# A second queue for the first weights: tile 1 of x sent behind tile 0, k's weights over two DMA queues, b1 and b2 sent after pair 10

## The chip, the cores and the metric

The kernel runs on one core of one Trainium2 chip. The metric is device time in microseconds, lower is better. The kernel before takes 485.36 us (median of three runs, 485.15 to 486.0). In the profile the engines are named PE (TensorE; PEld is its weight load), DVE (VectorE), ACT (ScalarE), POOL (GpSimd) and SP (SyncE). DMA transfers are issued by SP and by ACT, each with a queue of its own: q1 is SP's and q10 ACT's. Both run on the core's 16 DMA engines.

## The reference

One layer over 2048 positions of width 512, all in fp32:

```python
xn = layernorm(x)                                   # over the last axis, no gain
q, k, v = split(xn @ wqkv)                          # 32 heads of 16
logits = einsum(q, k at pos - 2*w, w = 0..7) / 4    # 8 keys, every second position back
attn = softmax(where(pos - 2*w >= 0, logits, -1e9))
s = einsum(attn, v at the same positions) @ wo
h = relu(xn @ w1 + b1) ** 2                         # 1792 hidden
g = silu(h @ w2 + b2)
out = x + s * g
```

x is (1, 2048, 512), wqkv (512, 1536), wo (512, 512), w1 (512, 1792), w2 (1792, 512), b1 (1792), b2 (512).

## The kernel before

**Precision.** Each large product is made of fast matmuls on a high part and a low part: every operand is split in two (`high` is a copy by ACT that rounds, `low` a subtraction), and three products (high by high, high by low, low by high) stand for one fp32 product. Only the very first product, k of tile 0, takes the fp32 operands as they are, so that it need not wait for splits.

**Phase 1, tiles of x.** x is cut into 16 tiles of 128 rows. A tile is loaded, normalized (statistics by `stats`: DVE, and rs by POOL; then `norm`), transposed, split, and multiplied by the weights of q, k and v. Tiles 0 and 1 are handled by code written out line by line; then come pairs of tiles, a = 2, 4, ... 14. Pairs 4 to 14 use sums of quarters of the tile and of the weights (`pair_of_seven`) to save a product. The q, k, v of a pair are stored to a scratch in DRAM (`store_qkv`: sq, sk, sv), from which attention loads units of 256 positions. Tiles from 4 on also store their transposed, split x to a scratch (sx), for phase 2.

**Attention** runs on DVE beside the products, as a stream of small steps which a planner lets in by estimated clocks of PE and DVE.

**Phase 2, the hidden layer.** For four chunks of 512 positions, blocks f = 0 to 13 of 128 hidden units: `up` makes h (ACT: relu with b1, then squares), `down` adds the product with w2 to four accumulators, which ACT filled with b2 before (`begin`). The first two blocks of chunk 0 lie already in pair 14. The weights of a block are loaded by `load_w` and split by `next_w`, two blocks ahead.

**The head.** The program starts with loads in this order: tile 0 of x, piece 0 of k's weights (rows 0 to 127 of the 512), tile 1, pieces 1 to 3 of k's weights, then q's weights in two halves, tiles 2 and 3, v's weights in two halves. Every one is issued by SP. PE meanwhile runs 18 transposes of the identity (tile `warm`). The chain to the first product is: tile 0 lands, bn_stats and bn_aggr on DVE, rs on POOL, xn in two halves on DVE, four transposes on PE (pxT), two copies on ACT (xT0f), and then k of tile 0 from xT0f and the raw pieces of the weights (pq from wqraw), the transposes of tile 1 between the third and the fourth piece.

**What sets the order.** Work on PE, DVE, ACT and POOL is written in the order in which each engine is to do it (`Ordered` keeps it). A transfer sent with `queue` or `A.dma_start` keeps its place too, on SP's and on ACT's queue. One sent with `dma` is placed by the scheduler: b1 and b2 stand in the code after pair 12 (line 885), but the scheduler issues them behind the first loads, since they wait for nothing. Each DMA issue also takes one of eight semaphores in turn, and waits until the transfer that had it eight issues earlier has landed.

Of the kernel before, what the change touches and what calls it, by code (L numbers as in the profile page):

```python
# [15 lines left out]
P = 128  # L16
S = 2048
D = 512
F = 1792
KT = D // P  # L20
# [39 lines left out]
def body(ctx: ExitStack, tc: tile.TileContext, x, wqkv, wo, w1, b1, w2, b2, out):  # L60
# [34 lines left out]
    PE, V, A, G = Ordered(nc.tensor, "PE"), Ordered(nc.vector, "V"), Ordered(nc.scalar), Ordered(nc.gpsimd)  # L95
# [4 lines left out]
    dma = nc.sync.dma_start  # L100

    def queue(out, in_):

        tc.keep_in_program_order(dma(out, in_))
# [19 lines left out]
    def piece(name):  # L124
        return keep.tile([P, 512], F32, name=name, tag="z", bufs=4)
# [26 lines left out]
    def load_x(t):  # L152
        xins[t] = px.tile([P, D], F32, name=f"x{t}", tag="x", bufs=4)
        queue(xins[t], tile_rows(x, t))
# [6 lines left out]

    raws = {}

    def load_wq(s, kt, tag=None):
        rows = wqkv[kt * P:(kt + (2 if tag else 1)) * P, s * 512:(s + 1) * 512]
        if tag is None:
            raws[s, kt] = piece(f"wqraw{s}_{kt}")
            dma(raws[s, kt], rows)
            return
        if kt == 0:  # L170
            raws[s] = att.tile([P, KT, 512], F32, name=f"wqraw{s}", tag=tag)
        dma(raws[s][:, kt:kt + 2], rows.rearrange("(k p) n -> p k n", p=P))
        for i in (kt, kt + 1):
            raws[s, i] = raws[s][:, i]
# [4 lines left out]


    load_x(0)
    load_wq(1, 0)
    load_x(1)
    for kt in range(1, KT):
        load_wq(1, kt)
    for kt in (0, 2):
        load_wq(0, kt, "pr")
    load_x(2)
# [17 lines left out]
    b1t = const.tile([P, NF], F32, name="b1t")  # L206
    b2t = const.tile([P, D], F32, name="b2t")
# [177 lines left out]
    def pump(margin=-SLACK):  # L385

        limit = clock["PE"] + margin
        flush(clock["PE"])
        while True:
            if coming[0] is None:  # L390
                coming[0] = next(stream, None)
            if coming[0] is None or clock["V"] + coming[0] > limit:
                break
            coming[0] = next(stream, None)
        if coming[0] is None:
            not_before(limit)
# [22 lines left out]
    NT = S // P  # L419
# [460 lines left out]
    for a in range(2, NT, 2):  # L880
        if a >= TPC:
            for t in (a, a + 1):
                queue(sx[t // TPC][:, :, t % TPC], xts[t].bitcast(F32))
        (pair_of_seven if a in SEVEN else pair)(a)
        if a == NT - 4:
            dma(b1t, b1.rearrange("(f p) -> p f", p=P))
            dma(b2t, b2[None, :].to_broadcast([P, D]))
    pump()
    lowh(1)
    p1ctx.close()  # L890
# [76 lines left out]
    for c in range(NCH):  # L967
# [7 lines left out]
        for f in range(2, NF):  # L975
# [4 lines left out]
            if c == 0 and f in (3, 6):  # L980
# [3 lines left out]
                for q in range(4):  # L984
                    rows = wo[q * P + 64 * i:q * P + 64 * i + 64, :].rearrange("(g p) n -> p g n", g=2)
# [105 lines left out]
```

## Time and profile before

| | before |
|---|---|
| median of 3 runs | 485.36 us (485.15 to 486.0) |
| profiled execution, its own time | 485.13 us |
| its span, first to last instruction | 483.1 us |
| granted TensorE clock | 1.00 |
| PE busy | 477.4 us (99%) |
| DVE busy | 423.0 us (88%) |
| first product of the kernel starts at | 6.70 us |
| DMA moved | 81.47 MB, mean 169 GB/s |

Times in the rows are microseconds from the span's start. A row of the timeline gives start, duration, engine, line, operation, the tile written, the tiles read, shapes, and the count where equal neighbours are merged; in brackets the idle time of that engine just before, and what ended it. L91 is the line of a helper through which nearly all instructions are issued, so rows are told apart by their tiles: `x` a tile of x, `wqraw` raw weights of q, k or v, `wq` their split, `st`, `mv`, `rs`, `xn` the steps of the normalization, `pxT` its transpose in PSUM, `xT0f` tile 0's transpose in fp32, `pq` and `pm` accumulators of q, k, v, `ph` and `pb` those of `up` and `down`, `stg` the stage of a store, `sx` the scratch of transposed x, `w1r` and `w2r` raw weights of phase 2. SPq and ACTq are DMA issues. The rows on which the argument rests stand in the prediction.

### The profile page before, as it was taken

What the parts mean: (1) busy time and instruction counts of PE and PEld (TensorE: products, weight loads), DVE (VectorE), ACT (ScalarE), POOL (GpSimd) and SP (SyncE); (2) the same over time, 40 slices, a digit from 0 to 9 for tenths busy, and PEclk for the clock granted to TensorE, in tenths of its full rate; (3) what the DMA queues carried; (4) which work ended last, traced back from release to release, by engine and by line L of the source; (5) the groups of instructions that cost most, each with busy time, mean ns of one, the idle gap of its engine ahead of it and who ended that gap; (6) DMA issues with size and microseconds to landing.
All of it is one profiled execution on the core that took longest, in us unless ns stands there. A gap on an engine that the chain in (4) does not pass through costs nothing.

```text
span 483.1 us, 6128 instructions
## 1 busy us (share of the span) xinstructions
PE 477.4 (99%) x2190; PEld 396.6 (82%) x2190; DVE 423.0 (88%) x352; ACT 240.0 (50%) x441; POOL 225.3 (47%) x178
## 2 busy tenths in 40 slices
PE   8999999999999999999999999999999999999996
PEld 5888888888888888888888888888888888888885
DVE  5978999899499899999999999999999999889133
ACT  5548798856566565273513345342234543423240
POOL 1459853116986699436543322434433345253210
PEclk9999999999999999999999999999999999999999
DMA  7899999998779996571627548071707725220321
GB/s 283 243 251 258 277 243 302 263 306 269 209 198 228 255 224 151 178 166 43 170 72 185 115 164 190 26 189 43 197 16 196 224 48 145 43 86 27 87 105 71
DMA packets 71002, 81.47 MB, mean 169 GB/s; under 512 B 6204, under 2 KB 55612, under 8 KB 70972
## 3 DMA queue, kind: packets, MB, share of 16 engines
q1 hardware_dynamic: 65788, 54.87, 41.3%
q10 hardware_dynamic: 5184, 26.22, 21.8%
q8 instruction: 17, 0.28, 0.2%
q14 instruction: 13, 0.11, 0.1%
HBM read 50.60 MB, written 27.32 MB: 161 GB/s over the span
## 4 chain that ended last, share of the span: by engine, by line
PE 98%; DMA 1%; DVE 0%; POOL 0%; issue 0%; ACT 0%; POOLq 0%
PE ph L91 32%; PE pb L91 32%; PE pm L91 12%; PE pq L91 9%; PE pw L91 9%; PE pv L91 4%; DMA x<-in_A_x 1%; PE pxT L91 0%; DVE z L91 0%; DVE st L91 0%; POOL rs L91 0%; DVE xn L91 0%; ACT xT0f L91 0%; DVE mv L91 0%; DVE rs L91 0%
## 5 line engine op out<-in xcount | busy, mean ns | idle before, releaser
L91 PE MATMUL pb<-w,h 128*128 128x512 f32 x672 | 160.1, 389 | 0.0
L91 PEld LDWEIGHTS pb<-w,h 128*128 128x128 f32 x672 | 126.1, 188 | 26.2
L91 POOL TENSOR_TENSOR h<-hf,h 128x512 fp32r<-128x512 f32 x46 | 67.7, 1473 | 157.5 <-ACT hf L91 157.5
L91 PE MATMUL ph<-xU,w 128*128 128x512 f32 x504 | 120.2, 389 | 0.0
L91 ACT ACTIVATE ph<-ph,b1t 128x512 f32<-128x512 f32 x56 | 37.0, 661 | 153.9 <-PE ph L91 144.0
L91 PEld LDWEIGHTS ph<-xU,w 128*128 128x128 f32 x504 | 94.6, 188 | 19.6
L91 DVE TENSOR_TENSOR pr<-k,q 128x2048 f32<-128x2048 f32 x32 | 78.7, 2460 | 3.2 <-DMA q<-sq 2.5
L91 DVE TENSOR_TENSOR pv<-v,L 128x2048 f32<-128x2048 f32 x32 | 77.3, 2417 | 3.8 <-POOL L L91 3.1
L91 DVE TENSOR_REDUCE L<-pr 128x128 f32<-128x2048 f32 x32 | 73.0, 2281 | 0.7
L91 DVE TENSOR_REDUCE v<-pv 128x256 f32<-128x2048 f32 x32 | 72.9, 2279 | 0.7
L91 PE MATMUL pw<-wot,oT 128*128 128x512 f32 (+1 forms) x204 | 45.9, 376 | 0.0
L91 PEld LDWEIGHTS pw<-wot,oT 128*128 128x128 f32 x204 | 36.8, 188 | 7.1
L91 POOL TENSOR_TENSOR w<-w1r,w 128x512 fp32r<-128x512 f32 x14 | 31.6, 2259 | 23.4 <-ACT w L91 23.2
L91 PE MATMUL ph<-xT,w 128*128 128x512 f32 x168 | 40.0, 389 | 0.0
L91 PEld LDWEIGHTS ph<-xT,w 128*128 128x128 f32 x168 | 31.5, 188 | 6.6
L91 PE MATMUL pm<-wq,S 128*128 128x512 f32 x144 | 36.8, 392 | 0.0
L91 ACT ACTIVATE h<-ph 128x512 fp32r<-128x512 f32 x56 | 33.5, 599 | 1.8
L91 PE MATMUL pq<-wq,xT 128*128 128x512 f32 x132 | 30.9, 393 | 0.0
L91 PEld LDWEIGHTS pm<-wq,S 128*128 128x128 f32 x144 | 26.2, 188 | 5.3 <-DVE S L91 0.4
L91 PEld LDWEIGHTS pq<-wq,xT 128*128 128x128 f32 x132 | 24.5, 188 | 5.9 <-ACT xT L91 0.7
L91 ACT ACTIVATE hf<-ph 128x512 f32<-128x512 f32 x46 | 27.4, 595 | 1.9 <-POOL h L91 1.9
L91 PE MATMUL pm<-wq,xt 128*128 128x512 f32 x108 | 27.6, 392 | 0.0
(96 smaller groups left out, 531.0 us busy)
## 6 DMA issues: line engine op xcount, KB each, us to landing
k<-sk ACTq DMA_DIRECT2D x8, 960.0 KB, 7.1
v<-sv ACTq DMA_DIRECT2D x8, 960.0 KB, 7.4
sx<-xt SPq DMA_DIRECT2D x12, 512.0 KB, 5.8
xU<-sx ACTq DMA_DIRECT2D x12, 512.0 KB, 5.9
x<-in_A_x SPq DMA_DIRECT2D x16, 256.0 KB, 6.4
sk<-stg SPq DMA_DIRECT2D x8, 512.0 KB, 4.3
sq<-stg SPq DMA_DIRECT2D x8, 512.0 KB, 7.5
sv<-stg SPq DMA_DIRECT2D x8, 512.0 KB, 5.0
```

Of the source, the lines that this page charges most:

```text
L91: return tc.keep_in_program_order(f(*a, **k))
```

## The change

Three things are altered:

1. Tile 1 of x is issued directly behind tile 0.
2. The four pieces of k's weights go out on two queues: pieces 0 and 2 are issued by ACT, pieces 1 and 3 by SP, each in a fixed place.
3. b1 and b2 are sent in a fixed place on SP's queue, after pair 10 (NT - 6), instead of by the scheduler from a place after pair 12.

```diff
-    def load_wq(s, kt, tag=None):
+    def load_wq(s, kt, tag=None, send=dma):
         rows = wqkv[kt * P:(kt + (2 if tag else 1)) * P, s * 512:(s + 1) * 512]
         if tag is None:
             raws[s, kt] = piece(f"wqraw{s}_{kt}")
-            dma(raws[s, kt], rows)
+            send(raws[s, kt], rows)
             return
...
     load_x(0)
-    load_wq(1, 0)
     load_x(1)
-    for kt in range(1, KT):
-        load_wq(1, kt)
+    for kt in range(KT):
+        load_wq(1, kt, send=queue if kt % 2 else A.dma_start)
...
         (pair_of_seven if a in SEVEN else pair)(a)
-        if a == NT - 4:
-            dma(b1t, b1.rearrange("(f p) -> p f", p=P))
-            dma(b2t, b2[None, :].to_broadcast([P, D]))
+        if a == NT - 6:
+            queue(b1t, b1.rearrange("(f p) -> p f", p=P))
+            queue(b2t, b2[None, :].to_broadcast([P, D]))
```

SP's first issues before. x_121 is tile 0 of x and x_125 tile 1, wqraw_0 to wqraw_3 are the four pieces of k's weights, wqraw_133 those of q:

```order
L104 DMA x_121<-in_A_x 128x512
L168 DMA wqraw_0_123<-in_A_wqkv 128x512
L104 DMA x_125<-in_A_x 128x512
L168 DMA wqraw_1_127<-in_A_wqkv 128x512
L168 DMA wqraw_2_129<-in_A_wqkv 128x512
L168 DMA wqraw_3_131<-in_A_wqkv 128x512
L172 DMA wqraw_133<-in_A_wqkv 128x2x512 x2
```

SP's first issues of the change (x_123 is now tile 1):

```order
L104 DMA x_121<-in_A_x 128x512
L104 DMA x_123<-in_A_x 128x512
L104 DMA wqraw_1_127<-in_A_wqkv 128x512
L104 DMA wqraw_3_131<-in_A_wqkv 128x512
L172 DMA wqraw_133<-in_A_wqkv 128x2x512 x2
```

Tile 1 moved up behind tile 0, and pieces 0 and 2 left SP's queue. They stand now at the start of ACT's instructions, where before the table load was first:

```order
L91 DMA wqraw_0_125<-in_A_wqkv 128x512
L91 DMA wqraw_2_129<-in_A_wqkv 128x512
L91 ACT_TABLE_LOAD
L91 ACTIVATE wq_113<-wqraw_0_125 128x512
L91 ACTIVATE xT0f<-pxT_0_169 128x256
```

ACT issues both pieces ahead of its table load, and its first work (the split of piece 0) stands behind it as before.

SP's queue before, from pair 10's store of q on. sx_154 is the scratch of transposed x of tiles 12 to 15 (four stores, of xt_1122, xt_1125, xt_1270 and xt_1273), w1r_1325 and w2r_1326 the weights of block 2, w1r_1416 and w2r_1417 those of block 3, and stg_1, stg_2, stg_0 pair 12's stages of k, v and q:

```order
L104 DMA sq<-stg_0_1088 128x8x128
L104 DMA sx_154<-xt_1122 512x1x256
L104 DMA sx_154<-xt_1125 512x1x256
L104 DMA sx_154<-xt_1270 512x1x256
L404 DMA w1r_1325<-in_B_w 128x4x128
L405 DMA w2r_1326<-in_B_w 128x512
L104 DMA sk<-stg_1_1234 128x8x128
L104 DMA sx_154<-xt_1273 512x1x256
L104 DMA sv<-stg_2_1235 128x8x128
L104 DMA sq<-stg_0_1236 128x8x128
L404 DMA w1r_1416<-in_B_w 128x4x128
L405 DMA w2r_1417<-in_B_w 128x512
```

The same place of the change, where the names of these tiles have other numbers (xt_1272 and xt_1275 are tiles 14 and 15, w1r_1327 and w2r_1328 block 2):

```order
L104 DMA b1t<-in_B_b 128x14x1
L104 DMA b2t<-in_B_b 128x512
L104 DMA sx_154<-xt_1122 512x1x256
L104 DMA sx_154<-xt_1125 512x1x256
L403 DMA w1r_1327<-in_B_w 128x4x128
L404 DMA w2r_1328<-in_B_w 128x512
L104 DMA sk<-stg_1_1236 128x8x128
L104 DMA sv<-stg_2_1237 128x8x128
L104 DMA sq<-stg_0_1238 128x8x128
L104 DMA sx_154<-xt_1272 512x1x256
L104 DMA sx_154<-xt_1275 512x1x256
L403 DMA w1r_1416<-in_B_w 128x4x128
```

b1 and b2 stand directly behind pair 10's store of q, and the stores of tiles 14 and 15 have gone behind all three stores of pair 12, directly ahead of the weights of block 3. On PE, DVE and POOL the order of the work is the same in both kernels.

## The prediction

> **What bounds the kernel now.** I read the page first: the busy shares, then the chain that ended last.
>
> ```profile
> span 483.1 us, 6128 instructions
> PE 477.4 (99%) x2190; PEld 396.6 (82%) x2190; DVE 423.0 (88%) x352; ACT 240.0 (50%) x441; POOL 225.3 (47%) x178
> PE 98%; DMA 1%; DVE 0%; POOL 0%; issue 0%; ACT 0%; POOLq 0%
> ```
>
> TensorE is the bound, and nearly alone. So the next question is where it is not working, which the waits of PE answer:
>
> ```profile
> PE warm L91 <- POOL mhalf L91: 1.4, 1, 1.4
> PE pxT L91 <- DVE xn L91: 0.3, 1, 0.3
> PE pq L91 <- ACT xT0f L91: 0.2, 1, 0.2
> ```
>
> These are all its waits in 483 us, and all lie at the start. A few microseconds before the first real product and after the last make the rest. So the change can act in two ways only: it moves the moment at which PE starts on real work, after which the dense stream shifts as a whole, or it makes PE wait somewhere for the first time. The chain in order of time, start us and duration, shows what sets that moment:
>
> ```profile
> 0.73 2.71 DMA x<-in_A_x
> ...
> 3.47 0.70 DVE st L91
> ...
> 5.31 0.42 DVE xn L91
> ...
> 5.78 0.46 PE pxT L91 x2
> ...
> 6.26 0.39 ACT xT0f L91
> ...
> 6.70 2.84 PE pq L91 x6
> ```
>
> From x's tile 0 landing to the first product there is no slack: statistics, rs, xn, four transposes, a copy. Whatever delays tile 0's landing delays everything; whatever lands later than tile 0 matters only if it becomes later than this chain.
>
> **Part 1, the head: tile 1 ahead, k's weights on two queues.** Today one queue carries tile 0, piece 0 of k's weights, tile 1, pieces 1 to 3, in that order. Issues and the waits that end on their landings:
>
> ```profile
> 0.73 0.39 SPq L104 DMA_DIRECT2D x<-in_A_x  x1
> 1.18 0.42 SPq L168 DMA_DIRECT2D wqraw<-in_A_wqkv  x1
> 1.65 0.42 SPq L104 DMA_DIRECT2D x<-in_A_x  x1
> 2.12 1.38 SPq L168 DMA_DIRECT2D wqraw<-in_A_wqkv  x3
> 0.73 1.28 ACT L91 ACT_TABLE_LOAD   x1 [0.73 <-PEq L1080]
> 3.47 0.69 DVE L91 BATCH_NORM_STATS2 st<-x 128x6 f32<-128x512 f32 x1 [3.47 <-DMA x<-in_A_x]
> 4.29 0.63 ACT L91 ACTIVATE wq<-wqraw 128x512 fp32r<-128x512 f32 x1 [2.28 <-DMA wqraw<-in_A_wqkv]
> 6.53 0.69 DVE L91 BATCH_NORM_STATS2 st<-x 128x6 f32<-128x512 f32 x1 [0.48 <-DMA x<-in_A_x]
> 7.23 0.19 PEld L91 LDWEIGHTS pq<-wqraw,xT0f 128*128 128x128 f32 x1 [0.24 <-DMA wqraw<-in_A_wqkv]
> 7.66 0.19 PEld L91 LDWEIGHTS pq<-wqraw,xT0f 128*128 128x128 f32 x1 [0.24 <-issue]
> 9.39 0.63 PE L91 MATMUL pxT<-ident,xn 128*128 128x128 f32 x4
> ```
>
> *What it gains.* Tile 1 lands at 6.5 and ends in its xn, which the transposes at 9.39 need. Ahead of them stand six half products in steps of 0.43 (7.66 - 7.23): the sixth's weights are loaded at 7.23 + 3 x 0.43 = 8.52, it starts a step later and gives way at 9.38. The transposes start at 9.39, and their row has no idle time. So tile 1 costs PE 0.01 or 0.02 us today, and an earlier tile 1 is worth no more: DVE is on xn of tile 0 until shortly before 6.5 in any case. SP also has two issues fewer ahead of its later ones (0.84 us); those bring the weights of q and tiles 2 and 3, for which PE waits in no row.
>
> *What it costs.* Piece 0 no longer stands behind tile 0 in one queue. It goes out on ACT's queue, and in the new order both of ACT's issues stand ahead of its table load, so the first can start at the 0.73 at which the table load starts now: the moment of tile 0's own issue. Two transfers of 256 KB then run side by side on the same 16 engines. Two bounds for what tile 0 loses:
> - Below, 0: tile 0 is served first and piece 0 gets the rest.
> - Above within fair sharing, 0.82: both are in by 4.29 today (4.29 - 3.47 = 0.82 after tile 0), and the last of the pair cannot land later if the same bytes move at the same rate.
>
> A tile of 128 rows of 2 KB is 8 pieces for each of 16 engines. If an engine takes pieces from the two queues in turn, tile 0's last is the 15th of 16 instead of the 8th: 7 of the 8 additional pieces stand ahead of it: 7/8 x 0.82 = 0.72. Is it in turn? The trace has one stretch where tiles of x on SP's queue and the load of q on ACT's share the engines, and one where SP's queue runs alone:
>
> ```profile
> DMA packets 163, 0.46 MB, mean 231 GB/s; under 512 B 7, under 2 KB 7, under 8 KB 163
> q10 hardware_dynamic: 76, 0.29, 59.9%
> q1 hardware_dynamic: 87, 0.18, 38.3%
> DMA packets 412, 0.78 MB, mean 389 GB/s; under 512 B 32, under 2 KB 32, under 8 KB 412
> DMA packets 325, 0.60 MB, mean 300 GB/s; under 512 B 32, under 2 KB 32, under 8 KB 325
> ```
>
> The first three rows are 33 to 35 us (q10 is ACT's queue, q1 SP's), the fourth 7 to 9 us, the last 2 to 4 us. With both queues loaded, 76 and 87 packets went through: about one for one. That is nearest to the fair share, so I take 0.72.
>
> [...]
>
> *What else moves.* ACT's table load starts 2 x 0.42 later and ends near 2.9; ACT's first work is at 4.29, so it is covered, and would cost only if the issues took 1.4 us longer than SP's. With the chain 0.72 later, DVE comes to tile 1's statistics at 6.77 instead of 6.53, so tile 1 may land 0.24 later than now without a wait. Piece 1 is now the third on SP, and the fifth transfer in the engines' common order instead of the fourth; it lands at 7.2 today, and one transfer more is up to 0.82, so at 8.0 or a little before, against a weight load that moves to 7.23 + 0.72 = 7.95. It fits without reserve; I put its price at 0, at most 0.2.
>
> **Part 2, b1 and b2 out of the head.** Both stand in SP's queue behind the first loads:
>
> ```profile
> 9.91 0.38 SPq L886 DMA_DIRECT2D b1t<-in_B_b  x1
> 11.27 4.25 SPq L887 DMA_DIRECT2D b2t<-in_B_b  x1
> 15.62 0.38 SPq L104 DMA_DIRECT2D sk<-stg  x1
> DMA packets 1978, 0.32 MB, mean 159 GB/s; under 512 B 1826, under 2 KB 1826, under 8 KB 1978
> ```
>
> b1 is 1,792 packets of 4 bytes (the last row, 15 to 17 us, shows them), b2 256 KB. Taking them away frees SP for about 4.6 us and the engines for some 2 us (I estimate 1.4 for b1, from the fall to 159 GB/s, and 0.65 for 256 KB at 389). Behind them stands the first store of k (15.62), which can leave earlier. Nothing of it reaches PE, which has no wait behind 6.7 us: gain 0.
>
> **Part 3, b1 and b2 after pair 10.** They now stand behind pair 10's store of q, and past them are queued the four stores of x^T, the weights w1 and w2 of block 2, and pair 12's stores:
>
> ```profile
> 102.21 4.05 SPq L104 DMA_DIRECT2D sq<-stg  x1
> 106.31 3.49 SPq L104 DMA_DIRECT2D sx<-xt  x3
> 114.08 0.38 SPq L404 DMA_DIRECT2D w1r<-in_B_w  x1
> 114.00:116.50 2.50, 2.50 (x15) 2.16 (x14) 2.43 (x4) 0.00 (x0) 2.50 (x3) 1.00 0.39 111
> 128.44 0.64 ACT L91 ACTIVATE ph<-ph,b1t 128x512 f32<-128x512 f32 x1
> 137.08 2.16 ACT L91 ACTIVATE pb<-b2t 128x512 f32<-128x512 f32 x4
> 127.12 0.63 ACT L91 ACTIVATE w<-w1r 128x512 fp32r<-128x512 f32 x1 [1.69 <-DMA w1r<-in_B_w]
> 132.93 0.60 ACT L91 ACTIVATE hf<-ph 128x512 f32<-128x512 f32 x1 [1.54 <-POOL h L91]
> ```
>
> SP has 4.3 us free between 109.8 and 114.08, and the fifth row (a window; its last columns are the DMA share 0.39 and 111 GB/s) shows the engines more than half idle at 114 to 116.5. b1 and b2 put 4.6 us into the first, less one store of x^T of 3.49 / 3 = 1.16 that goes behind pair 12's q now: net 3.5. They fit, 0.8 to spare. First uses are at 128.4 and 137.1, some 10 us after any plausible landing. The place to watch is 127.12: ACT waits there for w1 of block 3, and one store of x^T more (512 KB, 1.35 us at 389 GB/s) now stands between pair 12's stores and it, so it may come 1.3 to 1.5 us later. Behind it ACT stands idle 1.54 us at 132.93, so the delay is used up before it meets PE. Price 0; if that cover were gone, up to 1.5.
>
> **The sum.** +0.72 - 0.02 + 0 + 0 = +0.70. The profiled execution took 485.13 us (span 483.1); +0.70 is 485.83. The median of the runs is 485.36, 0.23 above that execution, so the forecast for the median is 486.06, rounded 486.1. Anything within 0.2% (0.97 us, about what a measurement of this kernel can tell from no change) counts as the same.
>
> **The rivals.**
> - *Shared queues are slower in sum.* At 33 to 35 us both queues together moved 231 GB/s, against 300 at 2 to 4 us and 389 at 7 to 9 us for SP's alone. If sharing itself costs that, 524 KB take 2.27 us instead of 1.75, and tile 0 lands 0.52 later still: +1.24 - 0.02, 486.6. It decides from a shared rate below about 262 GB/s (524 KB in 2.0 us, +0.97). Against it: the load of q in that stretch reads another memory layout than these loads do, and may be slow by itself.
> - *Tile 0 stays whole.* SP's pieces are in the engines first, and piece 0 takes only what they leave. Then the head is as before but for the 0.02: 485.36 - 0.02, 485.3. It needs ACT's first issue to start later than SP's by as much as tile 0 takes, or an engine that does not change queues within 8 pieces. The one-for-one count speaks against the second, but over 2 us it cannot show turns of 8.
>   [...]
> - *b1 and b2 find no room* (+0.5 to +1.5 at 128 to 139 us; 486.4): the spare above is 0.8 us on SP.
> - *Faster.* Two queues keep the engines busier at 2 to 4 us (300 GB/s, where 389 is possible): 524 KB would take 1.35 instead of 1.75, and tile 0 would lose 0.3 instead of 0.72, 485.7. For a real gain tile 0 would have to land before its 3.47, and nothing in the change sends it earlier; the most to win is PE's two waits, 0.5 us: 484.9.
>
> **How the numbers follow.** Forecast (tile 0 loses 0.3 to 0.97): 0.48. Slow sharing: 0.27. Tile 0 whole: 0.14. b1 and b2 in the way: 0.06. Faster: 0.05. Slower by over 0.2% takes slow sharing, half of the b1 case, and the upper edge of the forecast (0.08): 0.38. The last case, as far as it can be worked out, stays within 0.2%; beyond it lies only what this profile does not show, and I leave faster by over 0.2% those 0.05. Same is the rest, 0.57. The range goes from 485.2 (tile 0 whole, with runs that spread by some tenths) to 487.1 (slow sharing, with piece 1 or b1 on top).
>
> **What would show it.** The first statistics of DVE at 4.1 to 4.2 instead of 3.47 with PE's first product at 7.4; packets of q10 among those of the first 2 us; tile 1's statistics without a wait; ACT's table load behind two issues; PE without a wait from 7.4 to the end, at 114 to 139 us above all. The forecast is wrong if the first statistics stay at 3.5 (tile 0 whole), come after 4.5 (slow sharing), or if PE shows a wait that this profile does not have.

## The result

The changed kernel takes 489.06 us (median of six runs, 487.47 to 490.18) against 485.72 (485.15 to 486.01) for the kernel before beside it: a ratio of 1.0069, 95% interval 1.0048 to 1.009. It is 3.3 us slower; the forecast was +0.7, with 487.1 as the upper end. The profiled execution took 489.67 us, 4.54 more than the profiled one of before.

The page of the changed kernel, its span, busy time and chain by engine:

```profile
span 487.9 us, 6126 instructions
PE 480.5 (98%) x2190; PEld 397.1 (81%) x2190; DVE 421.5 (86%) x352; ACT 239.9 (49%) x441; POOL 238.5 (49%) x178
...
PE 85%; POOL 4%; DMA 4%; DVE 3%; issue 3%; ACT 1%; ACTq 0%; SPq 0%; DVEq 0%; POOLq 0%
```

PE was 98% of the chain that ended last and is 85%: POOL, DMA and DVE now stand on it. The waits of PE, and of its weight loads, name two places:

```profile
PE warm L91 <- POOL mhalf L91: 1.4, 1, 1.4
PE pxT L91 <- DVE xn L91: 1.2, 1, 1.2
PE ph L91 <- DVE h L91: 0.7, 1, 0.7
PEld ph L91 <- DVE h L91: 3.1, 6, 1.1
```

The wait ahead of the first transposes (pxT) has grown from 0.33 to 1.21 us, and there are six waits of the hidden layer's weight loads for DVE's h, one of which PE's own row shows too; the profile of before has none of them.

Where the 4.54 us lie can be cut at two instructions that both programs have: the first split product (pq from wq and xT) and the first hidden product (ph from xT). The timeline of PE gives their starts, here of before and then of the changed kernel:

```profile
10.71 3.04 PE L91 MATMUL pq<-wq,xT 128*128 128x512 f32 x12
...
123.99 4.24 PE L91 MATMUL ph<-xT,w 128*128 128x512 f32 x18
```

```profile
13.04 1.20 PE L91 MATMUL pq<-wq,xT 128*128 128x512 f32 x4
...
126.22 1.98 PE L91 MATMUL ph<-xT,w 128*128 128x512 f32 x8
```

The head costs 13.04 - 10.71 = 2.33 us. From there to the first hidden product it is 113.18 against 113.28. From the first hidden product to the start of the last product of the program the traces have 357.50 against 354.99: 2.51 us more. The start of the last product to the end of the span differs by 0.03, and the rest (-0.2) lies outside the span of the profile. So two losses, each of over 2 us in this execution, where one of 0.7 was forecast.

**The head.** The timeline of the changed kernel:

```profile
0.73 0.87 SPq L104 DMA_DIRECT2D x<-in_A_x  x2
0.73 0.89 ACTq L91 DMA_DIRECT2D wqraw<-in_A_wqkv  x2
1.66 1.28 ACT L91 ACT_TABLE_LOAD   x1 [1.66 <-PEq L1079]
4.35 0.69 DVE L91 BATCH_NORM_STATS2 st<-x 128x6 f32<-128x512 f32 x1 [4.35 <-DMA x<-in_A_x]
6.67 1.11 PE L91 MATMUL pxT<-ident,xn 128*128 128x128 f32 x4 [1.21 <-DVE xn L91]
6.85 0.69 DVE L91 BATCH_NORM_STATS2 st<-x 128x6 f32<-128x512 f32 x1
7.83 4.09 PE L91 MATMUL pq<-wqraw,xT0f 128*128 128x512 f32 x6
```

and the DMA view of 0.7 to 4.3 us, packets, MB and share by queue (q1 is SP's, q10 ACT's):

```profile
q1 hardware_dynamic: 234, 0.45, 39.6%
q10 hardware_dynamic: 160, 0.29, 23.3%
```

ACT's first issue does go out at 0.73, together with tile 0's. By the time tile 0 is in, the other queue has moved 160 packets beside SP's 234, where before SP's queue was alone. Tile 0's statistics begin at 4.35 instead of 3.47: 0.88 later, the step that the prediction put at 0.72. The view reaches a little past tile 0; from 0.7 to 3.7 us it has 137 packets of q1 and 116 of q10. The two queues together were also slower than the one queue of before, 234 against 284 GB/s at 1.7 to 3.5 us. But the products then lose more: the first six, 2.84 us before, take 4.09, and the four transposes 1.11 instead of the 0.76 that they took in the kernel before:

```profile
5.78 0.76 PE L91 MATMUL pxT<-ident,xn 128*128 128x128 f32 x4 [0.33 <-DVE xn L91]
```

The view of these products gives the shortest, median and longest of the eight in ns, of before and then of the changed kernel:

```profile
L91 PE MATMUL pq<-wqraw,xT0f x8: 592/592/697, 6.7 to 10.3; 128*128 128x512 f32 x8
```

```profile
L91 PE MATMUL pq<-wqraw,xT0f x8: 592/594/1220, 7.8 to 12.6; 128*128 128x512 f32 x8
```

The same product at up to twice the time, with no row of a wait ahead of it: the clock is the suspect.

**The middle.** In the rows below, of the changed kernel, first ACT, then SP, POOL, DVE and PE, SP sends two stores of x^T (sx) at 122.04, directly ahead of block 3's weights:

```profile
131.31 0.63 ACT L91 ACTIVATE w<-w1r 128x512 fp32r<-128x512 f32 x1 [4.24 <-DMA w1r<-in_B_w]
...
147.56 0.52 ACTq L91 DMA_DIRECT2D k<-sk  x1
...
157.87 0.52 ACTq L91 DMA_DIRECT2D q<-sq  x1
158.50 0.66 ACT L91 ACTIVATE ph<-ph,b1t 128x512 f32<-128x512 f32 x1 [8.80 <-DMA w2r<-in_B_w]
```

```profile
122.04 3.72 SPq L104 DMA_DIRECT2D sx<-xt  x2
...
148.70 0.34 SPq L404 DMA_DIRECT2D w2r<-in_B_w  x1
```

```profile
145.32 3.35 POOL L91 TENSOR_TENSOR w<-w2r,w 128x512 fp32r<-128x512 f32 x1
```

```profile
160.37 0.69 DVE L91 TENSOR_TENSOR h<-ph,h 128x512 fp32r<-128x512 f32 x1 [4.92 <-ACT ph L91]
...
161.12 3.03 PE L91 MATMUL ph<-xT,w 128*128 128x512 f32 x12 [0.70 <-DVE h L91]
```

And in the kernel before, the same two loads of ACT and the load of w2 of SP:

```profile
145.35 0.52 ACTq L91 DMA_DIRECT2D k<-sk  x1
...
147.77 0.52 ACTq L91 DMA_DIRECT2D q<-sq  x1
```

```profile
144.13 0.34 SPq L405 DMA_DIRECT2D w2r<-in_B_w  x1
```

```profile
142.81 1.29 POOL L91 TENSOR_TENSOR w<-w2r,w 128x512 fp32r<-128x512 f32 x1
```

The last row is POOL's split just ahead of that load. Read as a chain, with times counted from the first hidden product (123.99 before, 126.22 now): ACT gets w1 of block 3 at 5.1 instead of 3.1. POOL's splits of the following blocks slip, and the one at 145.32 takes 3.35 us where its counterpart of before took 1.29. That split frees the buffer for the load of w2 of block 7, which SP so issues at 22.5 instead of 20.1 (148.70, 0.03 us after the split's end at 148.67; before 144.13, after 144.10). At 21.3, in both kernels, ACT issues attention's load of k, 960 KB. Before, w2 went ahead of it; now it goes behind, and the DMA view of 150 to 152 us shows ACT's queue alone:

```profile
q10 hardware_dynamic: 60, 0.46, 100.0%
```

In the kernel before the same two microseconds have 52 packets of q10 and 51 of q1, so a load of k does not always keep SP's queue out; what decides is open.

ACT's next load, of q, takes one of the eight semaphores in turn, the one that this w2 still holds. So it is issued at 31.7 instead of 23.8, when w2 has landed (9.2 us after its issue at 148.70); ACT works in order and stands 8.80 us, DVE gets ph late (4.92), and PE waits for h (at 161.12, and five times more until 190). This is the reading of one execution; how far it holds is shown by the experiments.

### The profile page after: what moved, and what is told of

The parts are those of the page before. It is cut to its first block, busy times and chain, and to the rows that moved or that the text cites. A ratio compares the mean times of both kernels' runs of the same rounds, so it can differ in the third digit from the quotient of the medians.

```text
span 487.9 us, 6126 instructions
## 1 busy us (share of the span) xinstructions
PE 480.5 (98%) x2190; PEld 397.1 (81%) x2190; DVE 421.5 (86%) x352; ACT 239.9 (49%) x441; POOL 238.5 (49%) x178
## 4 chain that ended last, share of the span: by engine, by line
PE 85%; POOL 4%; DMA 4%; DVE 3%; issue 3%; ACT 1%; ACTq 0%; SPq 0%; DVEq 0%; POOLq 0%
PE pb L91 27%; PE ph L91 26%; PE pm L91 10%; PE pw L91 9%; PE pq L91 8%; PE pv L91 4%; DMA w2r<-in_B_w 3%; POOL w L91 3%; DVE L L91 1%; DMA x<-in_A_x 1%; POOL stg L91 1%; DVE h L91 1%; ACT ph L91 1%; DVE pv L91 0%; PE pxT L91 0%
## 5 line engine op out<-in xcount | busy, mean ns | idle before, releaser
L91 POOL TENSOR_TENSOR h<-hf,h 128x512 fp32r<-128x512 f32 x46 | 76.6, 1666 | 145.5 <-ACT hf L91 143.0
L91 DVE TENSOR_TENSOR pr<-k,q 128x2048 f32<-128x2048 f32 x32 | 77.7, 2429 | 1.3 <-DMA q<-sq 0.6
L91 POOL TENSOR_TENSOR w<-w1r,w 128x512 fp32r<-128x512 f32 x14 | 36.0, 2572 | 22.1 <-ACT w L91 22.1
```

The source lines that it names most:

```text
L91: return tc.keep_in_program_order(f(*a, **k))
```

## The experiments

Each is told against the kernel before in runs on the same chip. In the profiles three numbers were compared: the start of the first split product (10.71 before), the moment of ACT's copy of block 3's w1 behind the first hidden product (3.1 before), and the time from the first hidden product to the last product (354.99 before).

**The two halves alone.** The head's two edits with b1 and b2 as before, and the move of b1 and b2 with the head as before. The diff of the second:

```diff
-        if a == NT - 4:
-            dma(b1t, b1.rearrange("(f p) -> p f", p=P))
-            dma(b2t, b2[None, :].to_broadcast([P, D]))
+        if a == NT - 6:
+            queue(b1t, b1.rearrange("(f p) -> p f", p=P))
+            queue(b2t, b2[None, :].to_broadcast([P, D]))
```

> Only the head of the change (tile 1 behind tile 0, k's pieces on two queues); b1 and b2 stay where the kernel before has them. Theory A (the loss is two: tile 0 lands 0.9 us late and the wider gap ahead of PE's transposes keeps TensorE's clock low, 2.3 us together at the head; and a separate stall at 160 to 190 us that comes from b1 and b2 standing among pair 10's and 12's stores): the first product of the k accumulator on split weights starts at about 13.0 instead of 10.7, no wait of PE behind 20 us, median about 487.7 (+2.0 to +2.4). Rival B (the stall at 160 us comes from the head's shift alone): the stall shows here too, about 489.5. Rival C (b1 and b2 make the head late): head as before, about 485.6.

> Only b1 and b2 are sent after pair 10; the head is as before. Theory A: first work on split weights at 10.7 as before; ACT waits for w1 of block 3 about 4 us instead of 1.7, the load of q behind 145 us is issued some 8 to 10 us later than before, and PE waits for DVE's low part of h between 155 and 190 us, in sum 2 to 2.4 us: 487.5 to 488. Rival B: no wait of PE at all, 485.4 to 486.

Head alone: 487.26 us against 486.55 (ratio 1.0014, 0.9991 to 1.0037). b1 and b2 alone: 487.66 (1.0018, 0.9997 to 1.0039). Neither is told from no change, and their sum, 0.32%, is not the 0.69% of the whole; in these runs the kernel before stood 0.8 to 1.2 us higher than in the others. The profiles say more. b1 and b2 alone: 10.71 as before, but the copy of w1 at 5.23 and 357.74 us to the end, so the stall in the middle comes without a late head. Head alone: statistics at 4.30, first split product at 12.73, and against the expectation a stall too: the copy of w1 at 4.09, waits of PE for h, 357.32 us to the end. Single profiles so do not tell which half carries the stall.

**Is the late tile 0 due to sharing?** In the changed kernel ACT does a one-column copy first, so that its table load stands ahead of its two issues:

```diff
-    for kt in range(KT):
-        load_wq(1, kt, send=queue if kt % 2 else A.dma_start)
+    for kt in (1, 3):
+        load_wq(1, kt, send=queue)
+    early = const.tile([P, 1], F32, name="early")
+    A.activation(early, ident[:, :1], AF.Copy)
+    for kt in (0, 2):
+        load_wq(1, kt, send=A.dma_start)
```

> The changed kernel, but ACT does a one-column copy first, so that its table load and that copy stand ahead of its two issues: pieces 0 and 2 go out at about 2.3 instead of 0.73, when most of tile 0 is through. Theory A (tile 0 is late because piece 0 shares the engines with it): tile 0 lands at 3.3 to 3.5 as before, the first product starts at 6.7 to 6.9, the head loses nothing, and what is left against the kernel before is the stall behind 155 us: 485.4 to 488. Rival E (tile 0 is late because tile 1 stands directly behind it on its own queue): still 4.2 to 4.4, and the head as in the changed kernel.

492.14 us (1.0111, 1.0084 to 1.0139), where at most 488 was expected. Tile 0's statistics are back at 3.34: without a transfer beside it tile 0 lands as before. But piece 0 comes so late that ACT, in order, holds back the copies of tile 0's transposes, and PE waits:

```profile
PE pq L91 <- ACT xT0f L91: 4.5, 1, 4.5
```

Stores of x^T stand in this kernel as in the changed one, yet there is no stall: the copy of w1 came at 3.92, and 354.99 us to the end. Why it came in time there is open.

**More warm products in the changed kernel** (WARM 22 instead of 18), to fill PE's idle time ahead of the transposes.

> The changed kernel with 22 transposes of the identity instead of 18 at the start (4 x 0.213 = 0.85 us more work for PE, which fills the added gap). Theory A (clock): tile 0 still lands 0.9 us late, but the transposes of tile 0 and the first products run at full speed (0.43 between the six half products instead of 0.77 to 1.01), the head loses 0.9 to 1.0 instead of 2.3, so about 1.3 us less than the changed kernel in the same call. Rival D (the slow first products come from late pieces of the weights, not from the clock): the same 0.77 to 1.01 between them, no gain.

487.86 us (1.0033, 1.0011 to 1.0055), against the 1.0069 of the changed kernel, which was not run beside it. The statistics still begin at 4.38, but the half products (the first six products of k of tile 0) are back at 2.84 and the first split product at 11.79 (timeline of PE). The middle still stalls (358.18 us to the end).

```profile
6.69 0.88 PE L91 MATMUL pxT<-ident,xn 128*128 128x128 f32 x4 [0.38 <-DVE xn L91]
7.83 2.84 PE L91 MATMUL pq<-wqraw,xT0f 128*128 128x512 f32 x6 [0.26 <-ACT xT0f L91]
...
11.79 2.55 PE L91 MATMUL pq<-wq,xT 128*128 128x512 f32 x10
```

**The stores of x^T moved out of the way**: tiles 14 and 15 stored in pair 14, behind the loads of blocks 3 to 5, in the changed kernel and in the kernel before; beside them the changed kernel and the kernel before once more, unaltered.

```diff
+    def store_x(t):
+        queue(sx[t // TPC][:, :, t % TPC], xts[t].bitcast(F32))
+    for t in (14, 15):
+        at(14, 3, store_x, t)
...
-        if a >= TPC:
+        if TPC <= a < NT - 2:
```

> The changed kernel once more, on the chip of the other runs of this call. The chain found in the traces so far: w1 of block 3 lands later after the first work of the hidden layer (5.1 us instead of 3.1), POOL's splits of the weights slip by half a microsecond into DVE's long operations and stretch from 1.3 to 3.35 us, the load of w2 of block 7 is issued behind ACT's load of k instead of ahead of it, the load of q waits for it 8 us in ACT's queue, and PE waits at 160 to 190 us. Theory: the same chain here, q's load more than 29 us after the first hidden work (23.8 in the kernel before), head 10.9 to 13.1, median 1.5 to 3.5 us above the kernel before in this call. Rival: the stall is an accident of the first call's execution and does not come back: 0.7 to 1.1 us above.

> The changed kernel with the two stores of x^T of tiles 14 and 15 moved behind the loads of blocks 3, 4 and 5, into step 3 of pair 14. Theory (the stall starts with w1 of block 3 standing behind those stores): w1 of block 3 lands at most 3.5 us after the first hidden work, q's load is issued at about 23.8, no wait of PE behind 100 us, and the time falls by 2 to 2.5 us against the changed kernel in this call; what is left is the head. Rival (b1 and b2 themselves, or the order of the semaphores, make the stall): still above 27 us for q's load, and no gain.

> The same move of the two stores in the kernel before. Theory: where the kernel before shows times of 487 and more, it has the same stall by its own scatter (w1 of block 3 lands at 3.1 us after the first hidden work, and about 4.0 is the point from which it stalls). With the stores out of the way the scatter above 487 goes, and the median falls below the kernel before in this call by up to 1 us, its best runs at 484.8 as before. Rival: the scatter of the kernel before comes from its head (the phase of the clock), and stays.

> The kernel before, unchanged, for a second profile of it. Theory: head as in the first (first split product at 10.7); if its time is above 487, the load of q behind 145 us is issued 27 us or more after the first hidden work and PE waits at 160 to 190 us; if it is near 485, at 23.8 and no wait.

The changed kernel again: 489.12 us (1.0069, 1.0048 to 1.009), 3.8 above the kernel before, a little more than expected. The stall came back, but weaker in the profiled execution: the copy of w1 at 4.95, 356.52 us to the end, and q's load issued at 26.7 behind the first hidden product, where more than 29 was expected. With the late stores 489.57 (1.0075, 1.0048 to 1.0102): the expected gain failed to come. The copy of w1 came at 1.5, as meant, but the loads of k and q were now late (k at 22.9), and DVE waited for q:

```profile
DVE pr L91 <- DMA q<-sq: 4.3, 1, 4.3
```

In the kernel before this wait is 2.5 us. 356.26 us to the end, with waits of PE's weight loads for h of 1.6 in sum: one wait seems traded for another. In the kernel before the same move costs 0.18% (1.0002 to 1.0035), 486.51 us, where a gain was expected. This edit was too blunt to say whether the stores are the cause.

The four profiles gave the clock away. The changed kernel again, in three windows (us, the busy time of PE, PEld, DVE, ACT, POOL, then the granted clock, DMA share, GB/s):

```profile
4.70:8.00 3.30, 1.65 (x9) 0.86 (x8) 2.42 (x9) 1.33 (x4) 0.60 (x2) 1.00 1.04 397
8.10:11.40 3.30, 3.30 (x5) 1.32 (x4) 2.75 (x5) 1.76 (x4) 0.81 (x1) 0.50 1.05 389
11.50:14.00 2.50, 2.50 (x12) 1.43 (x11) 0.84 (x2) 1.21 (x3) 0.00 (x0) 1.00 1.04 385
```

Here the clock had risen at 4.59. In the 3.41 us from there on, in which PE stood idle 1.50 us, it was still full; in the next 3.41 (8.01 to 11.42), though PE was busy all through, it was 0.50. (Ahead of its first record the view shows 1.00 too, also for 8.10 to 10.37 us of the changed kernel's first profile, where weight loads come in steps of 0.85 us.) The trace's complete records of the clock are multiples of 3.41 us long (3.41 us at 0.50 here, 477.87 us, which is 140 times 3.413, in the first profiles of the kernel before and of the changed kernel), and their start differs from execution to execution (5.64 and 10.37 us in those two). That 1.50 us of idle time lowered the clock for the next 3.41 us is the reading of this one execution.

In the first profile of the changed kernel the clock did not fall, it rose late: its first record begins at 10.37. The weight loads of the half products come in steps of 0.85 us ahead of it and of 0.43 behind it (timeline of PEld):

```profile
9.69 0.34 PEld L91 LDWEIGHTS pq<-wqraw,xT0f 128*128 128x128 f32 x1 [0.52 <-issue]
...
10.90 0.19 PEld L91 LDWEIGHTS pq<-wqraw,xT0f 128*128 128x128 f32 x1 [0.24 <-issue]
```

3.41 us earlier would have been 6.96, and PE's idle 1.21 us (5.46 to 6.67) lie in the 3.41 us that ended there; that the clock moves in such steps is an estimate from the lengths of its records. Three other profiles with a wide gap show a late rise too, at 9.80 to 10.85, with half products of 3.83 to 4.36 us instead of 2.84.

The changed kernel with the late stores shows another case: same idle time of 1.21, clock up at 5.67 and not down again, and the first split product at 11.54. There the head costs 11.54 - 10.71 = 0.83, the sharing alone:

```profile
6.66 0.76 PE L91 MATMUL pxT<-ident,xn 128*128 128x128 f32 x4 [1.21 <-DVE xn L91]
7.58 2.84 PE L91 MATMUL pq<-wqraw,xT0f 128*128 128x512 f32 x6 [0.15 <-ACT xT0f L91]
...
11.54 2.79 PE L91 MATMUL pq<-wq,xT 128*128 128x512 f32 x11
```

And the kernel before, run once more (486.99), had the late clock without any change: its half products took 4.66 us, its first split product came at 12.67, where 10.7 was expected, and its clock rose at 10.58; the middle had no stall (354.99). Its gap was 0.27 us, less than the 0.38 of the changed kernel with 22 warm products, whose clock rose at 7.19. So the length of the gap is not all that decides; what else does is open.

**The clock by itself.** The kernel before with 14 warm products, which widens the idle time and touches no transfer; and with 20, which fills it:

```diff
-WARM = 18
+WARM = 14
```

> The kernel before with 14 warm products instead of 18 and no transfer touched, so PE's idle time ahead of the first transposes of x grows from 0.33 us to 1.2 us (four products at 0.23 us), as wide as in the changed kernel. Clock theory (the wider gap delays the rise of the clock): the first products run longer, the dense stream begins at 12 to 13 us in the profile instead of 10.71, and the median is 0.5 to 2 us above the kernel before. Rival (only the late arrival of the k weights and of tile 0 moved the dense stream): 10.7 and the same time within 0.3 us.

> The kernel before with 20 warm products instead of 18: PE's idle time ahead of the first transposes (0.33 us) is filled, and the transposes begin about 0.13 us later. Clock theory: fewer executions with a late rise of the clock, a median 0.1 us later to 0.5 us earlier than the kernel before. Rival (the clock does not look at this gap): 0.1 to 0.2 us slower in every execution.

With 14: 487.37 us against 485.51 (1.0026, 1.0009 to 1.0043). The timeline of PE:

```profile
5.69 1.12 PE L91 MATMUL pxT<-ident,xn 128*128 128x128 f32 x4 [1.08 <-DVE xn L91]
6.85 4.36 PE L91 MATMUL pq<-wqraw,xT0f 128*128 128x512 f32 x6
...
12.33 3.92 PE L91 MATMUL pq<-wq,xT 128*128 128x512 f32 x16
```

Four warm products fewer, in time that nobody uses, cost 1.3 us (0.26% of 485.5). So the wider gap alone has a price. With 20: 486.33 (1.0005, 0.9989 to 1.002), which tells neither a gain nor a loss; that filling the gap of the kernel before helps is not shown. Over all profiles: with an idle time of 1.08 to 1.50 us the half products were slow in five of six (3.83 to 4.54 us against 2.84), with 0.55 or less in two of nine (4.66 in the kernel before once more, and 4.73 in the reorder below), the kernel with the late piece 0 left out.

**b1 and b2, or the order of the stores?** Moving b1 and b2 also moved two stores of x^T: in the kernel before, those of tiles 14 and 15 stand ahead of block 2's weights and amid pair 12's stores; in the changed kernel both stand behind pair 12's stores. Two kernels part the two, both with the head of before. The first has this reorder and nothing else (seven rows of SP's order; b1 and b2 are sent by the same plain sends from a place ahead of the pair loop, and stay where they were). The second moves b1 and b2 and keeps the stores' places:

```diff
         if a >= TPC:
             for t in (a, a + 1):
-                queue(sx[t // TPC][:, :, t % TPC], xts[t].bitcast(F32))
+                (dma if a == NT - 2 else queue)(sx[t // TPC][:, :, t % TPC], xts[t].bitcast(F32))
```

> The kernel before with one thing changed, seven rows of SP's order: the stores of x^T of tiles 14 and 15 stand behind the three pair 12 stores, directly ahead of block 3's weights, as they do in the changed kernel; b1 and b2, the head and all rows of the other four engines are as before. Theory A (this reorder, a by-product of taking the plain sends of b1 and b2 out of pair 12, makes the stall in the middle): ACT's copy of block 3's w1 begins 4 us or more behind the first hidden product (before 3.13), PE waits of about 1 us and then 0.3 to 0.5 us stand between 160 and 190, from the first hidden product to the last product 356 to 358 us instead of 354.99, and the time is 1 to 2.5 us above the kernel before. Theory B (the 256 KB of b1 and b2 at pair 10 make it): 354.99 as before, the same time within 0.3 us.

> The kernel before with b1 and b2 sent behind pair 10 as in the changed kernel, and the stores of x^T of tiles 14 and 15 at the places that they have in the kernel before, so that of the second half of the change only the two loads of b1 and b2 are moved. Theory A (the reorder of the stores makes the stall): copy of block 3's w1 3.1 to 3.9 us behind the first hidden product, 354.99 us from there to the end, no waits of PE, the same time as before within 0.3 us. Theory B (the traffic of b1 and b2): the copy at 4 us or later, waits between 160 and 190, 1 to 2.5 us slower.

The reorder alone: 487.19 us against 485.51 (1.0032, 1.0012 to 1.0051). b1 and b2 alone: 485.58 (1.0002, 0.9988 to 1.0016). The timelines of ACT, of the reorder and then of b1 and b2:

```profile
131.01 0.63 ACT L91 ACTIVATE w<-w1r 128x512 fp32r<-128x512 f32 x1 [4.27 <-DMA w1r<-in_B_w]
...
155.98 0.52 ACTq L91 DMA_DIRECT2D q<-sq  x1
```

```profile
127.49 0.63 ACT L91 ACTIVATE w<-w1r 128x512 fp32r<-128x512 f32 x1 [1.77 <-DMA w1r<-in_B_w]
...
150.23 0.55 ACTq L91 DMA_DIRECT2D q<-sq  x1
```

The copy comes 5.1 and 3.2 us behind the first hidden product. That the cause is the reorder and not the traffic of b1 and b2 is what the medians say, though the two intervals just touch: seven of twelve executions took 487 us or more with the reorder, four of twelve with b1 and b2 alone. One expectation was not met: the profiled execution of the second kernel (487.45, among its longer ones) also waits, 2.5 us in PE's weight loads, and takes 356.99 us to the end, with the copy on time and w2 ahead of k. So a late copy is not the only way into the stall; that w2's landing beside k's 960 KB varies from execution to execution is a likely reason, not a shown one. The reorder makes the bad case the more frequent one. In the six profiles with the reorder the copy of w1 came at 4.9 to 5.2 in five, which took 356.5 to 358.2 us, and at 3.92 in the one without a stall. In the eight that had the old order it came at 3.1 to 4.1, with 354.99 in three, 355.9 to 357.3 in five, the worst of them the one at 4.1. The head does not sort these eight: without a stall it ended at 10.71, 10.87 and 12.67, with one at 10.57 to 13.29.

**Does it add up?** The changed kernel with the old order of the stores, and the same with all four pieces of k's weights on SP behind tile 1:

```diff
-        load_wq(1, kt, send=queue if kt % 2 else A.dma_start)
+        load_wq(1, kt, send=queue)
```

> The changed kernel with the stores of x^T of tiles 14 and 15 back at the places in SP's order that they have in the kernel before; head, b1 and b2 as changed. Theory (the loss is the sum of a head part and of the reorder of these stores): the stall of 1.5 us or more goes, the head part stays: 1 to 2.2 us above the kernel before, 486.5 to 487.7, against 489.1 for the changed kernel; first statistics at 4.3 us, dense stream at 11.5 to 13.2, copy of block 3's w1 at most 3.9 us behind the first hidden product. Rival (head and middle are not separate, the late head brings the stall by itself): 488.5 or more.

> The same, and the four pieces of k's weights all on SP behind the two tiles of x, so that nothing shares the engines with tile 0. What stays of the change is tile 1 ahead of piece 0 and the place of b1 and b2. Theory (the head part comes from the piece on ACT's queue that shares with tile 0, and from the clock that the wider gap delays): first statistics back at 3.4 us, idle time ahead of the first transposes 0.33 us, dense stream at 10.6 to 11 us, 485.2 to 485.9, the time of the kernel before within 0.4 us. Rival (the order of tile 1 and piece 0 costs by itself, since piece 0 lands 0.7 us later): dense stream 0.5 us or more later and the median 0.5 to 1 us above.

Without the reorder: 487.64 us against 485.63 (1.0035, 1.0015 to 1.0055), with the copy of w1 at 3.25 and still 355.95 us to the end in the profile. 0.35% for the head and 0.32% for the reorder make 0.67%, beside the 0.69% that was measured; with intervals of 0.2% either way on each, so close a sum is partly luck. The changed kernel with the reorder and without it (1.0069 and 1.0035) points to the reorder as the pair above does. With one queue as well: 486.77 (1.0012, 0.9995 to 1.0029), not told from no change; what it adds is not settled, since the interval reaches to +0.29% while its profiled execution, 485.29 us, has the head of before but for 0.16 us:

```profile
5.74 1.11 PE L91 MATMUL pxT<-ident,xn 128*128 128x128 f32 x4 [0.28 <-DVE xn L91]
6.90 2.84 PE L91 MATMUL pq<-wqraw,xT0f 128*128 128x512 f32 x6
...
10.87 5.31 PE L91 MATMUL pq<-wq,xT 128*128 128x512 f32 x22
```

No kernel beat the one before.

## Why the prediction was wrong, step by step

- *Tile 0 shares the engines, +0.72*: right. The statistics came 0.88 late, and where the clock was up the head lost 0.83. The packet counts, 137 to 116, say nearly one for one. "Tile 0 stays whole" fell, since tile 0 came late. The counts here do not part the engines, so they cannot tell whether one engine divided tile 0. "Slow sharing" fell by its own sign, since 4.35 is short of 4.5, but had a part, since both queues together moved 234 GB/s at 1.7 to 3.5 us and the one queue of before 284.
- *The chain behind tile 0 keeps its length* (first product at 7.4, the stream shifted by 0.70): wrong, and this is the first step that failed. It was never written as a term. The products came at 7.83 and ran at about half speed until 10.37 (weight loads 0.85 us apart, 0.43 behind it): 0.83 became 2.33 in the profile. The prediction let a longer wait of PE at the start cost its length and no more; it also bears on whether the clock is up when the work begins: with 1.08 us of it instead of 0.33, and no transfer touched, the half products took 4.36 us instead of 2.84. The median price of the gap is 1.3 us (the kernel with 14 warm products).
- *Tile 1 earlier gains 0.02, piece 1 fits, the table load is covered*: nothing contradicts it. Tile 1's statistics did not wait (6.85), and the table load went behind the issues (1.66) without delaying ACT.
- *Part 2, nothing gained*: right for the head, as the kernel with only b1 and b2 moved shows (1.0002).
- *Part 3, price 0*: the second step that failed. The place named was the right one: block 3's w1 did come late, by 1.95 us against the 1.3 to 1.5 expected. What failed was "ACT stands idle 1.54 at 132.93, so the delay is used up before it meets PE". ACT's idle time was looked at and not POOL's next splits; in the changed kernel's profile these delayed the next weight loads past the load of k, and PE got the waits that the prediction had named as a sign of being wrong. The cover was checked for one engine at one place; the delay left it through another. Nor was the price at stake 1.5: in the executions with the stall it is 1.5 to 3.2, and 1.6 in the median.
- *The rival "b1 and b2 find no room"* had about the right size and place, but the wrong cause: their traffic costs nothing that can be told (1.0002, 0.9988 to 1.0016). The stores of tiles 14 and 15, which the diff does not name, do.
- *The sum*: 0.35% for the head and 0.32% for the reorder against the 0.14% forecast.

## What to carry to other kernels

At the start, an idle gap of PE must be priced twice: its length, and what the clock does in the next few microseconds (0.50 for 3.41 us here, behind a gap of 1.50). Warm products should leave no wide gap ahead of the first real work: a gap of 1.08 us instead of 0.33 cost 1.3 us here, while filling the 0.33 showed no gain. When a delay is said to be covered, follow every engine that takes work from the delayed one, up to the next large transfer that it may fall behind. And compare the whole order of a queue, not only the moved rows: taking the plainly sent b1 and b2 out of their place let the scheduler place two stores anew, and these cost as much as the whole head.

## What the runs showed of the hardware

- In the second profile of the changed kernel PE stood idle 1.50 us while the clock was full (4.59 to 8.01 us), and the clock was 0.50 for the next 3.41 us, though PE was busy all that time. In four other executions a gap of 1.08 to 1.24 us went with a rise of the clock at 9.80 to 10.85 us instead of 4.59 to 7.19. In a sixth, with 1.21, the clock was up at 5.67 and stayed up.
- With gaps up to 0.55 us the clock, once up, stayed up. But in two of nine such executions, with gaps of 0.27 and 0.22 us, it came up only at 10.58 and 10.67, and the length of the gap does not tell these two from the others. So one and the same kernel has its first split product at 10.71 or at 12.67.
- In the first profile of the changed kernel, beside a load of 960 KB on ACT's queue, SP's queue moved nothing for a while: from 150 to 152 us all 60 packets were ACT's, though SP had issued w2 at 148.70. In the kernel before the two queues moved 52 and 51 packets in the same stretch, beside the same load. At 0.7 to 3.7 us, with loads of 256 KB on both queues, the changed kernel's moved 137 (SP's) and 116.
- Of POOL's 56 splits of weights of the hidden layer in the first profiles of the kernel before and of the changed kernel, 34 take 1.28 to 1.30 us, 20 take 3.04 to 3.44 us and two lie between (1.88 and 2.45). Each of the 22 longer ones runs beside a product of two tiles on DVE (128x2048), and none is longer that has only DVE's sums of that length beside it, or nothing. Nine that overlap such a product by 0.05 to 0.87 us stay short, and this was not tried apart.
